# Reordering the attention steps beside an MLP's column blocks, with the first loads in halves (Trainium2, one core)

## The chip, the cores and the metric

One core of a Trainium2 chip runs the whole kernel. The metric is the device time of one execution in microseconds, lower is better. A profile of one more execution shows the engines: TensorE (PE, with weight loads as PEld), VectorE (DVE), ScalarE (ACT), GpSimd (POOL), SyncE (SP) and the DMA queues.

## The reference

```python
q, k, v: (8, 8, 576, 64)   # batch, heads, sequence, head size
kv = einsum('bhsd,bhse->bhde', k, v)
o  = einsum('bhsd,bhde->bhse', q, kv)
o  = o / sqrt(mean(o*o, -1) + 1e-6) * g_norm       # per head
x  = o.transpose(0, 2, 1, 3).reshape(4608, 512)
h  = x @ w_in                                      # 512 -> 2048
g  = max(h, 0) + alpha * min(h, 0)
out = g @ w_out                                    # 2048 -> 512, float32
```

Linear attention (no softmax) over 576 positions, a norm per head, and an MLP with a PReLU over all 4608 tokens.

## The kernel before

The 4608 tokens are cut into nine windows of 512 (`W`). A window needs the normed attention output transposed, 512 channels in four tiles of 128 (`xt`, one for each pair of heads), and then runs sixteen column blocks, called groups (`g`, 128 of the 2048 hidden columns each).

**The MLP.** `m1_group` (L325) runs four h matmuls (L310), one for each `xt` tile, into one of three PSUM buffers `h`; ScalarE makes `m_sb` (L317) and VectorE `gt` (L319) out of it. The y matmuls (`y_mm`, L332) of a window run one window later, four in each group beside the h matmuls; `y_out` copies a finished tile with ScalarE (L339) and sends it off. Window 0 is different: its h groups run alone (L367), and its y matmuls then run in a block of their own (L379), into four PSUM tiles `ya` to `yd`, three of which are `h` buffers.

**The attention.** For a batch b and a pair of heads j there are four steps. `step_t` transposes q (five matmuls, L222) into `qt_ps`, and VectorE copies it to `qt_sb` (L231). `step_kv` multiplies k and v (five matmuls, L237) into `kv_ps`, and VectorE masks it to `kv_sb` (L245). Both use the same single PSUM buffer (`ps_s`, tag "s"). `step_ot` multiplies both (L256) into `ot_ps` (two buffers), and ScalarE squares it (`sq_sb`, L262). `step_ssq` sums the squares (L268, one PSUM buffer); ScalarE takes Ln and Exp (L270, L273) and VectorE multiplies to `xt` (L275).

**The order.** Each engine works through its own instructions in the order in which the program was written (`manual_schedule`). `step_stream` (L280) gives the steps of all windows in one sequence: ot j-1, t j, ssq j-1, kv j. `attn_step` takes the next one. In windows 1 to 8 one step is taken behind each group (L406), so the sixteen steps for window w+1 end behind group 15 of window w. In the first y block one or two are taken behind each group from group 6 on. At the start, `keep_warm` (L198) puts matmuls whose result is not used between the steps.

**The loads.** GpSimd issues all loads of q, k, v and the weights, in one order. `load_main` brings 512 of a batch's 576 positions into a stage tile (two per tensor), `load_rem` the other 64 straight to their place; `regroup` copies the stage tile into the layout of the steps, on VectorE, ScalarE or GpSimd. For batch 0 the loads and regroups go by pairs of heads; the regroups of batch 1 are on VectorE (L371), and those of batch 2 and later on GpSimd, behind their loads.

Of the kernel before, what the change touches and what calls it, by code (L numbers as in the profile page):

```python
# [17 lines left out]
def kernel(  # L18
# [161 lines left out]

    for j in range(NPAIR):
        for nm in ("k", "v", "q"):
            load_main(0, nm, 2 * j, 2 * j + 2)
            if j == 0:
                load_rem(0, nm)
    for i in range(WQ):
# [7 lines left out]
    load_batch(2)  # L194
    regroup_batch(2)

# [20 lines left out]

    def step_t(b, j):
        qs = bufs[b % NBUF]["q"]
        qt_ps = ps_s.tile([P, NT * P], FP16, name="qt_ps", tag="s")  # L220
        for t in range(NT):
# [10 lines left out]

    def step_kv(b, j):
        ks, vs = bufs[b % NBUF]["k"], bufs[b % NBUF]["v"]
        kv_ps = ps_s.tile([P, P], FP32, name="kv_ps", tag="s")
        for t in range(NT):
            nc.tensor.matmul(  # L237
                out=kv_ps[:],
                lhsT=ks[:, t, 2 * j : 2 * j + 2, :],
                rhs=vs[:, t, 2 * j : 2 * j + 2, :],  # L240
                start=(t == 0),
                stop=(t == NT - 1),
            )
        kvs[b, j] = attn_p.tile([P, P], FP16, name="kv_sb", tag=f"kv{j}")
        nc.vector.tensor_mul(out=kvs[b, j][:], in0=kv_ps[:], in1=mask32[:])  # L245
# [33 lines left out]

    def step_stream():  # L280
        for w in range(NW):
            new = w < B
            for j in range(NPAIR + 1):
                if j > 0:
                    yield w, lambda: step_ot(w, j - 1)
                if new and j < NPAIR:
                    yield w, lambda: step_t(w, j)
                if j > 0:
                    yield (w + 1 if j == NPAIR else w), lambda: step_ssq(w, j - 1)
                if new and j < NPAIR:  # L290
                    yield w, lambda: step_kv(w, j)

    stream = step_stream()
    windows_done = 0

    def attn_step():
        nonlocal windows_done
        nxt = next(stream, None)
        if nxt is None:
            return False  # L300
        nxt[1]()
        windows_done = nxt[0]
        return True

# [49 lines left out]

    for j in range(NPAIR):
        regroup(0, "k", 2 * j, 2 * j + 2)
        regroup(0, "v", 2 * j, 2 * j + 2, nc.scalar)
        regroup(0, "q", 2 * j, 2 * j + 2)
        n = 3 if j == 0 else 4
        for _ in range(n):  # L360
            attn_step()
            keep_warm(2)
    while windows_done < 1:
        attn_step()
        keep_warm(1)

    for g in range(NF):  # L367
        m1_group(0, g)


    for nm in ("k", "v", "q"):  # L371
        regroup(1, nm, 0, H)
# [4 lines left out]
        ps_h.tile([P, W], FP32, name="yd", tag="h"),  # L377
    ]
    for g in range(NF):  # L379
        for a in range(TPW):  # L380
            y_mm(ys[a], 0, a, g)
        if g >= 6:
            attn_step()
        if g >= 10:
            attn_step()
    for a in range(TPW):
        y_out(ys[a], 0, a)
    while windows_done < 2:
        attn_step()

    for w in range(1, NW):
        if w + 2 < B:
            load_batch(w + 2)
            regroup_batch(w + 2)
        y = None
        for g in range(NF):
            m1_group(w, g)
            if w > 1:
# [5 lines left out]
                if part == TPW - 1:  # L404
                    y_out(y, w - 1, a)
            attn_step()  # L406
        while windows_done < min(w + 2, NW):
            attn_step()
    for a in range(TPW):
# [34 lines left out]
```

## Time and profile before

| | |
|---|---|
| runs of the kernel before | 339.92, 340.24, 340.5 us; median 340.24 |
| the profiled execution | 339.78 us, its span 338.0 us |
| TensorE busy | 300.1 us, 89% |
| VectorE busy | 159.7 us, 47% |
| ScalarE busy | 174.8 us, 52% |
| GpSimd busy | 84.3 us, 25% |
| granted TensorE clock, mean | 0.988 |

The span runs from the first to the last instruction. A matmul of 512 columns shows as 380 ns from its issue to its end, but the next one starts long before that; so what counts on TensorE is the distance of starts and the idle time ahead of an instruction, in brackets, with what ended it.

### The profile page before, as it was taken

The numbers are of one execution on the slowest core, as the hardware profiler recorded it, in microseconds if no ns is written. First come the engines' busy times: TensorE is split into PE (matmuls) and PEld (weight loads), VectorE is DVE, ScalarE is ACT, GpSimd is POOL, SyncE is SP. The second block draws the span as 40 slices with busy tenths as digits, with TensorE's granted clock in tenths as the row PEclk, the third lists the DMA queues.
The fourth block names the chain that finished last, engine by engine and source line by source line (L and its number), as shares of the span: only waits on it lengthen the run. The fifth ranks groups of instructions, "written<-read, shape, count | busy, mean of one in ns | idle before, by whom it ended". The sixth has DMA issues, their size and how long they took to land.

```text
span 338.0 us, 4258 instructions
## 1 busy us (share of the span) xinstructions
PE 300.1 (89%) x1614; PEld 143.8 (43%) x1614; DVE 159.7 (47%) x272; ACT 174.8 (52%) x293; POOL 84.3 (25%) x89
## 2 busy tenths in 40 slices
PE   5768998487779997999899989998998899999994
PEld 1333444243334544554454445444444444444441
DVE  5445842347645554554455445544554555444400
ACT  2356604557646664566456646563656684444411
POOL 9943417585752053305420000000000000000000
PEclk9799999989999999999999999999999999999999
DMA  8999997999391159204921111100001112100042
GB/s 79 171 204 200 197 195 91 157 190 178 40 178 39 31 64 195 46 32 65 192 48 33 31 31 33 31 33 32 31 33 31 31 32 49 46 31 33 32 94 62
DMA packets 47717, 28.07 MB, mean 83 GB/s; under 512 B 14400, under 2 KB 43088, under 8 KB 47696
## 3 DMA queue, kind: packets, MB, share of 16 engines
q0 software_dynamic: 42000, 18.35, 43.9%
q1 hardware_dynamic: 5696, 9.45, 9.9%
q8 instruction: 12, 0.20, 0.3%
q14 instruction: 9, 0.07, 0.1%
HBM read 36.71 MB, written 9.44 MB: 137 GB/s over the span
## 4 chain that ended last, share of the span: by engine, by line
PE 80%; ACT 9%; DVE 5%; POOL 2%; DMA 2%; issue 1%; POOLq 0%; ACTq 0%
PE h_ps L310 34%; PE y_ps L332 33%; DVE xt L275 3%; ACT rstd L270 3%; ACT rstd L273 3%; PE ot_ps L256 3%; PE qt_ps L222 3%; PE kv_ps L237 2%; PE ssq_ps L268 2%; DMA qst<-in_q_dram 2%; ACT y_sb L339 1%; ACT m_sb L317 1%; DVE gt L319 1%; PE yd L332 1%; PE ya L332 1%
## 5 line engine op out<-in xcount | busy, mean ns | idle before, releaser
L310 PE MATMUL h_ps<-xt,w_in_sb 128*128 128x512 f16 x576 | 147.6, 382 | 14.8 <-DVE xt L275 12.4
L319 DVE SCALAR_TENSOR_TENSOR gt<-m_sb,beta_sb,h_ps 128x512 f16<-128x512 f32 x144 | 107.4, 746 | 97.0 <-ACT m_sb L317 95.1
L332 PE MATMUL y_ps<-w_out_sb,gt 128*128 128x512 f16 x512 | 128.8, 379 | 0.0
L317 ACT ACTIVATE m_sb<-h_ps 128x512 f32<-128x512 f32 x144 | 85.3, 594 | 83.7 <-PE h_ps L310 83.2
L332 PEld LDWEIGHTS <-gt 128*128 128x128 f16 x576 | 55.9, 98 | 79.0 <-issue 14.0
L310 PEld LDWEIGHTS <-w_in_sb 128*128 128x128 f16 x576 | 54.0, 98 | 57.7 <-issue 6.1
L275 DVE SCALAR_TENSOR_TENSOR xt<-ot_ps,g2col,rstd 128x512 f16<-128x512 f32 x36 | 27.0, 751 | 46.4 <-ACT rstd L273 46.4
L262 ACT ACTIVATE sq_sb<-ot_ps 128x512 f16<-128x512 f32 x36 | 21.5, 597 | 35.7 <-PE ot_ps L256 35.5
L270 ACT ACTIVATE rstd<-ssq_ps,eps_t 128x512 f32<-128x512 f32 x36 | 24.8, 688 | 14.4 <-PE ssq_ps L268 14.4
L339 ACT COPY y_sb<-y_ps 128x512 f32<-128x512 f32 x32 | 18.7, 585 | 19.0 <-PE y_ps L332 19.0
L256 PE MATMUL ot_ps<-qt_sb,kv_sb 128*128 128x512 f16 (+7 forms) x64 | 15.2, 292 | 11.5 <-DVE kv_sb L245 11.5
L273 ACT ACTIVATE rstd<-rstd 128x512 f32<-128x512 f32 x36 | 22.7, 629 | 1.1
L231 DVE COPY qt_sb<-qt_ps 128x576 f16<-128x576 f16 x32 | 14.5, 453 | 10.0 <-PE qt_ps L222 10.0
L222 PE MATMUL qt_ps<-ident,qsb 128*128 128x128 f16 x160 | 14.5, 223 | 2.4 <-DVE qsb L139 2.2
L201 PE MATMUL warm_ps<-warm,mask 128*128 128x512 f16 x41 | 14.3, 454 | 2.3 <-DVE warm L95 2.3
L222 PEld LDWEIGHTS <-qsb 128*128 128x128 f16 x160 | 11.6, 99 | 10.7 <-DVE qsb L139 3.9
L139 POOL COPY ksb<-kst 128x2048 f16<-128x2048 f16 x6 | 11.4, 1893 | 18.2 <-DMA kst<-in_k_dram 18.2
L256 PEld LDWEIGHTS <-kv_sb 128*128 128x128 f16 x64 | 6.2, 97 | 21.9 <-DVE kv_sb L245 15.7
L237 PEld LDWEIGHTS <-ksb 128*128 128x128 f16 x160 | 11.7, 99 | 8.4 <-DVE qt_sb L231 0.6
L128 POOL DMA_DIRECT2D ksb<-in_k_dram x8 | 5.7, 713 | 37.5 <-PE kv_ps L237 35.7
L237 PE MATMUL kv_ps<-vsb,ksb 128*128 128x128 f16 x160 | 14.4, 222 | 0.4 <-DVE qt_sb L231 0.3
L268 PE MATMUL ssq_ps<-sq_sb,mask 128*128 128x512 f16 x36 | 13.7, 380 | 0.9 <-ACT sq_sb L262 0.9
(44 smaller groups left out, 126.5 us busy)
## 6 DMA issues: line engine op xcount, KB each, us to landing
out_dram<-y_sb SPq DMA_DIRECT2D x40, 128.0 KB, 2.3
out_dram<-y_sb SPq DMA_DIRECT2D x16, 256.0 KB, 2.2
kst<-in_k_dram POOLq DMA_DIRECT2D x7, 512.0 KB, 6.3
vst<-in_v_dram POOLq DMA_DIRECT2D x7, 512.0 KB, 8.8
qst<-in_q_dram POOLq DMA_DIRECT2D x7, 512.0 KB, 10.8
w_in_sb<-in_moe_w_in_dram POOLq DMA_DIRECT2D x4, 512.0 KB, 9.5
w_out_sb<-in_moe_w_out_dram POOLq DMA_DIRECT2D x4, 512.0 KB, 15.9
kst<-in_k_dram POOLq DMA_DIRECT2D x4, 128.0 KB, 4.8
```

Of the source, the lines that this page charges most:

```text
L222: nc.tensor.matmul(out=qt_ps[:, t * P : (t + 1) * P], lhsT=qs[:, t, 2 * j : 2 * j + 2, :], rhs=ident16[:], is_transpose=True, start=(t == ...
L237: nc.tensor.matmul(out=kv_ps[:], lhsT=ks[:, t, 2 * j : 2 * j + 2, :], rhs=vs[:, t, 2 * j : 2 * j + 2, :], start=(t == 0), stop=(t == NT - 1),)
L256: nc.tensor.matmul(out=ot_ps[:, n0 - w * W : n1 - w * W], lhsT=kvs[b, j][:], rhs=qts[b, j][:, n0 - b * S : n1 - b * S], start=True, stop=True,
L262: nc.scalar.activation(out=sq[:], in_=ot_ps[:], func=AF.Square)
L270: nc.scalar.activation(out=rstd[:], in_=ssq_ps[:], func=AF.Ln, bias=eps_t[:], scale=inv_d,)
L273: nc.scalar.activation(out=rstd[:], in_=rstd[:], func=AF.Exp, bias=0.0, scale=-0.5)
L275: nc.vector.scalar_tensor_tensor(out=xts[w, j][:], in0=ot_ps[:], scalar=g2col[:], in1=rstd[:], op0=ALU.mult, op1=ALU.mult,)
L310: nc.tensor.matmul(out=h_ps[:], lhsT=w_in_blk(c, g), rhs=xts[w, c][:], start=(c == 0), stop=(c == NC - 1),)
L317: nc.scalar.activation(out=m_sb[:], in_=h_ps[:], func=AF.Relu, scale=-1.0)
L319: nc.vector.scalar_tensor_tensor(out=gt[:], in0=m_sb[:], scalar=beta_sb[:, g : g + 1], in1=h_ps[:], op0=ALU.mult, op1=ALU.add,)
L332: nc.tensor.matmul(out=y[:], lhsT=gts[w, g][:, a * P : (a + 1) * P], rhs=w_out_blk(g), start=(g == 0), stop=(g == NF - 1),)
L339: nc.scalar.copy(out=y_sb[:], in_=y[:])
```

## The change

The sequence of the steps is written anew (`window_steps`): t j, ot j-1, kv j, ssq j-1, and the steps for window w+1 all stand in window w, spread so that the last comes behind group 13 instead of behind group 15. In window 1 they begin behind group 4. In the first y block steps stand between y matmuls, half a group apart, and end in group 14. Batch 0 is loaded in two halves of four heads, the remainders between them; the steps of two pairs run together, with three of their PSUM tiles taken from the `h` buffers, and the first three groups of window 0 run their matmuls for the early heads before the late heads are there. The regroup of batch 2 moves from GpSimd to VectorE, into window 1, and the load of batch 3 moves behind it in the program. Fewer `keep_warm` matmuls run at the start (10 + 10 instead of 10 + 31).

```diff
@@ -178,11 +178,12 @@
         i, r = divmod(g, GW)
         return w_out_sb[i][:, r, :]
 
-    for j in range(NPAIR):
-        for nm in ("k", "v", "q"):
-            load_main(0, nm, 2 * j, 2 * j + 2)
-            if j == 0:
-                load_rem(0, nm)
+    for nm in ("k", "v", "q"):
+        load_main(0, nm, 0, H // 2)
+    for nm in ("k", "v", "q"):
+        load_rem(0, nm)
+    for nm in ("k", "v", "q"):
+        load_main(0, nm, H // 2, H)
     for i in range(WQ):
         load_w_in(i)
     load_batch(1, ("k",))
@@ -192,7 +193,6 @@
     load_w_out(2)
     load_w_out(3)
     load_batch(2)
-    regroup_batch(2)
 
 
     def keep_warm(n):
@@ -215,9 +215,9 @@
 
     qts, kvs, xts = {}, {}, {}
 
-    def step_t(b, j):
+    def step_t(b, j, pool=(ps_s, "s")):
         qs = bufs[b % NBUF]["q"]
-        qt_ps = ps_s.tile([P, NT * P], FP16, name="qt_ps", tag="s")
+        qt_ps = pool[0].tile([P, NT * P], FP16, name="qt_ps", tag=pool[1])
         for t in range(NT):
             nc.tensor.matmul(
                 out=qt_ps[:, t * P : (t + 1) * P],
@@ -230,9 +230,9 @@
         qts[b, j] = attn_p.tile([P, S], FP16, name="qt_sb", tag=f"qt{j}")
         nc.vector.tensor_copy(out=qts[b, j][:], in_=qt_ps[:, 0:S])
 
-    def step_kv(b, j):
+    def step_kv(b, j, pool=(ps_s, "s")):
         ks, vs = bufs[b % NBUF]["k"], bufs[b % NBUF]["v"]
-        kv_ps = ps_s.tile([P, P], FP32, name="kv_ps", tag="s")
+        kv_ps = pool[0].tile([P, P], FP32, name="kv_ps", tag=pool[1])
         for t in range(NT):
             nc.tensor.matmul(
                 out=kv_ps[:],
@@ -277,30 +277,20 @@
             op0=ALU.mult, op1=ALU.mult,
         )
 
-    def step_stream():
-        for w in range(NW):
-            new = w < B
-            for j in range(NPAIR + 1):
-                if j > 0:
-                    yield w, lambda: step_ot(w, j - 1)
-                if new and j < NPAIR:
-                    yield w, lambda: step_t(w, j)
-                if j > 0:
-                    yield (w + 1 if j == NPAIR else w), lambda: step_ssq(w, j - 1)
-                if new and j < NPAIR:
-                    yield w, lambda: step_kv(w, j)
-
-    stream = step_stream()
-    windows_done = 0
-
-    def attn_step():
-        nonlocal windows_done
-        nxt = next(stream, None)
-        if nxt is None:
-            return False
-        nxt[1]()
-        windows_done = nxt[0]
-        return True
+    def window_steps(w):
+        f = []
+        for j in range(NPAIR):
+            f.append(("t", j))
+            if j > 0:
+                f.append(("ot", j - 1))
+            f.append(("kv", j))
+            if j > 0:
+                f.append(("ssq", j - 1))
+        f += [("ot", NPAIR - 1), ("ssq", NPAIR - 1)]
+        if w >= B:
+            f = [x for x in f if x[0] in ("ot", "ssq")]
+        fn = {"t": step_t, "kv": step_kv, "ot": step_ot, "ssq": step_ssq}
+        return [lambda n=n, j=j: fn[n](w, j) for n, j in f]
 
 
     gts = {}
@@ -352,23 +342,38 @@
             i += cnt
 
 
-    for j in range(NPAIR):
-        regroup(0, "k", 2 * j, 2 * j + 2)
-        regroup(0, "v", 2 * j, 2 * j + 2, nc.scalar)
-        regroup(0, "q", 2 * j, 2 * j + 2)
-        n = 3 if j == 0 else 4
-        for _ in range(n):
-            attn_step()
-            keep_warm(2)
-    while windows_done < 1:
-        attn_step()
-        keep_warm(1)
-
-    for g in range(NF):
+    H_POOL = (ps_h, "h")
+    for j0 in (0, 2):
+        regroup(0, "q", 2 * j0, 2 * j0 + 4)
+        regroup(0, "v", 2 * j0, 2 * j0 + 4, nc.scalar)
+        regroup(0, "k", 2 * j0, 2 * j0 + 4)
+        j1 = j0 + 1
+        step_t(0, j0, H_POOL)
+        step_t(0, j1, H_POOL)
+        step_kv(0, j0)
+        step_kv(0, j1, H_POOL)
+        step_ot(0, j0)
+        step_ot(0, j1)
+        if j0 == 0:
+            keep_warm(4)
+            step_ssq(0, j0)
+            step_ssq(0, j1)
+            keep_warm(6)
+    first = [ps_h.tile([P, W], FP32, name="h_ps", tag="h") for g in range(3)]
+    for g in range(3):
+        m1_mm(first[g], 0, g, (0, 1))
+    step_ssq(0, 2)
+    step_ssq(0, 3)
+    for g in range(3):
+        m1_mm(first[g], 0, g, (2,))
+    for g in range(3):
+        m1_mm(first[g], 0, g, (3,))
+        m1_evac(first[g], 0, g)
+    for g in range(3, NF):
         m1_group(0, g)
 
 
-    for nm in ("k", "v", "q"):
+    for nm in ("q", "k", "v"):
         regroup(1, nm, 0, H)
     ys = [
         ps_y.tile([P, W], FP32, name="ya", tag="y"),
@@ -376,24 +381,31 @@
         ps_h.tile([P, W], FP32, name="yc", tag="h"),
         ps_h.tile([P, W], FP32, name="yd", tag="h"),
     ]
+    steps = window_steps(1)
     for g in range(NF):
         for a in range(TPW):
             y_mm(ys[a], 0, a, g)
-        if g >= 6:
-            attn_step()
-        if g >= 10:
-            attn_step()
+            if g >= 6 and steps and (a == 1 or (a == 3 and g >= 8)):
+                steps.pop(0)()
     for a in range(TPW):
         y_out(ys[a], 0, a)
-    while windows_done < 2:
-        attn_step()
+    for f in steps:
+        f()
 
     for w in range(1, NW):
-        if w + 2 < B:
+        steps = window_steps(w + 1) if w + 1 < NW else []
+        n = len(steps)
+        first_g = 4 if w == 1 else 0
+        if 1 < w and w + 2 < B:
             load_batch(w + 2)
             regroup_batch(w + 2)
         y = None
         for g in range(NF):
+            if w == 1 and g == first_g - 1:
+                for nm in ("q", "k", "v"):
+                    regroup(2, nm, 0, H)
+                load_batch(3)
+                regroup_batch(3)
             m1_group(w, g)
             if w > 1:
                 a, part = divmod(g, TPW)
@@ -403,9 +415,10 @@
                     y_mm(y, w - 1, a, gg)
                 if part == TPW - 1:
                     y_out(y, w - 1, a)
-            attn_step()
-        while windows_done < min(w + 2, NW):
-            attn_step()
+
+            want = n * (g - first_g + 1) // (NF - 2 - first_g)
+            while steps and n - len(steps) < want:
+                steps.pop(0)()
     for a in range(TPW):
         y = ps_h.tile([P, W], FP32, name="y_ps", tag="h")
         for g in range(NF):
```

TensorE behind the last group that has attention steps, in window 2. First before (behind group 15; the rows at the end are window 3's group 0), where L332 are y matmuls, L268 is ssq and L310 are h matmuls:

```order
L332 LDWEIGHTS gt
L332 MATMUL y_ps<-w_out_sb_178,gt 128x512
L268 LDWEIGHTS mask_106
L268 MATMUL ssq_ps<-sq_sb,mask_106 128x512
L310 LDWEIGHTS w_in_sb_155
L310 MATMUL h_ps<-xt,w_in_sb_155 128x512
```

and of the change, behind group 13 of window 2 (L256 is ot 3, L300 are h matmuls):

```order
L322 LDWEIGHTS gt
L322 MATMUL y_ps<-w_out_sb_162,gt 128x512
L256 LDWEIGHTS kv_sb
L256 MATMUL ot_ps<-qt_sb,kv_sb 128x192
L256 LDWEIGHTS kv_sb
L256 MATMUL ot_ps<-qt_sb,kv_sb 128x320
L268 LDWEIGHTS mask_106
L268 MATMUL ssq_ps<-sq_sb,mask_106 128x512
L300 LDWEIGHTS w_in_sb_155
L300 MATMUL h_ps<-xt,w_in_sb_155 128x512
```

The last ssq stands two groups earlier, and directly behind the ot that it needs.

VectorE in the first y block (qt copy L231, kv_sb L245, xt L275), before, from the regroup of batch 1 on:

```order
L231 COPY qt_sb<-qt_ps 128x576
L245 TENSOR_TENSOR kv_sb<-kv_ps,mask_102 128x128
L231 COPY qt_sb<-qt_ps 128x576
L275 SCALAR_TENSOR_TENSOR xt<-ot_ps,g2col,rstd 128x512
L245 TENSOR_TENSOR kv_sb<-kv_ps,mask_102 128x128
L231 COPY qt_sb<-qt_ps 128x576
L275 SCALAR_TENSOR_TENSOR xt<-ot_ps,g2col,rstd 128x512
L245 TENSOR_TENSOR kv_sb<-kv_ps,mask_102 128x128
```

and of the change:

```order
L231 COPY qt_sb<-qt_ps 128x576
L245 TENSOR_TENSOR kv_sb<-kv_ps,mask_102 128x128
L231 COPY qt_sb<-qt_ps 128x576
L245 TENSOR_TENSOR kv_sb<-kv_ps,mask_102 128x128
L275 SCALAR_TENSOR_TENSOR xt<-ot_ps,g2col,rstd 128x512
L231 COPY qt_sb<-qt_ps 128x576
L245 TENSOR_TENSOR kv_sb<-kv_ps,mask_102 128x128
L275 SCALAR_TENSOR_TENSOR xt<-ot_ps,g2col,rstd 128x512
```

kv_sb j+1 now stands ahead of xt j, and the qt copy of pair j+2 behind it.

VectorE at the start of window 1, of the change (gt L309, regroup of batch 2 L139); before, these three copies were GpSimd's:

```order
L309 SCALAR_TENSOR_TENSOR gt<-m_sb,beta_sb,h_ps 128x512 x3
L139 COPY qsb_135<-qst 128x8x4x64
L139 COPY ksb_131<-kst 128x8x4x64
L139 COPY vsb_133<-vst 128x8x4x64
L309 SCALAR_TENSOR_TENSOR gt<-m_sb,beta_sb,h_ps 128x512 x2
L231 COPY qt_sb<-qt_ps 128x576
L309 SCALAR_TENSOR_TENSOR gt<-m_sb,beta_sb,h_ps 128x512
L245 TENSOR_TENSOR kv_sb<-kv_ps,mask_102 128x128
L231 COPY qt_sb<-qt_ps 128x576
```

The first qt copy of the window's steps stands behind three copies and gt 4, and kv_sb 0 and the second qt copy follow with one gt between.

## Rows read from the trace of the kernel before

**Rows 1.** Whom TensorE waited for in the whole span: us in total, times, longest us.

```profile
PE h_ps L310 <- DVE xt L275: 12.4, 7, 1.8
PE ot_ps L256 <- DVE kv_sb L245: 11.5, 9, 1.3
```

**Rows 2.** TensorE's timeline, windows 2 and 3: start us, us, engine, line, [idle before <-releaser].

```profile
94.88 0.38 PE L310 MATMUL h_ps<-xt,w_in_sb 128*128 128x512 f16 x1 [1.84 <-DVE xt L275]
...
121.66 0.44 PE L237 MATMUL kv_ps<-vsb,ksb 128*128 128x128 f16 x5
121.94 1.03 PE L310 MATMUL h_ps<-xt,w_in_sb 128*128 128x512 f16 x4
122.81 1.03 PE L332 MATMUL y_ps<-w_out_sb,gt 128*128 128x512 f16 x4
123.67 0.38 PE L256 MATMUL ot_ps<-qt_sb,kv_sb 128*128 128x192 f16 x2
...
125.83 0.81 PE L310 MATMUL h_ps<-xt,w_in_sb 128*128 128x512 f16 x3
128.49 0.38 PE L310 MATMUL h_ps<-xt,w_in_sb 128*128 128x512 f16 x1 [1.85 <-DVE xt L275]
```

**Rows 3.** Busy time by stage, first y block and window 1: us, engines, granted clock, DMA.

```profile
41.68:68.13 26.45, 18.95 (x117) 9.34 (x116) 8.99 (x17) 9.26 (x16) 13.33 (x12) 0.98 1.22 150
68.13:95.10 26.97, 20.93 (x121) 10.17 (x120) 16.68 (x28) 16.95 (x30) 18.29 (x17) 0.95 0.96 139
```

**Rows 4.** Timeline of all engines, one pair in the first y block.

```profile
57.36 0.38 PE L268 MATMUL ssq_ps<-sq_sb,mask 128*128 128x512 f16 x1
...
57.78 0.69 ACT L270 ACTIVATE rstd<-ssq_ps,eps_t 128x512 f32<-128x512 f32 x1 [0.76 <-PE ssq_ps L268]
...
58.50 0.63 ACT L273 ACTIVATE rstd<-rstd 128x512 f32<-128x512 f32 x1
...
59.83 0.28 DVE L245 TENSOR_TENSOR kv_sb<-kv_ps,mask 128x128 f16<-128x128 f32 x1
...
60.85 0.46 DVE L231 COPY qt_sb<-qt_ps 128x576 f16<-128x576 f16 x1 [0.74 <-PE qt_ps L222]
```

**Rows 5.** Timeline of all engines, end of the first y block.

```profile
64.31 0.36 PE L256 MATMUL ot_ps<-qt_sb,kv_sb 128*128 128x448 f16 x1 [1.25 <-DVE kv_sb L245]
...
64.71 0.60 ACT L262 ACTIVATE sq_sb<-ot_ps 128x512 f16<-128x512 f32 x1 [1.44 <-PE ot_ps L256]
65.36 0.38 PE L268 MATMUL ssq_ps<-sq_sb,mask 128*128 128x512 f16 x1 [0.69 <-ACT sq_sb L262]
...
68.13 1.44 PE L310 MATMUL h_ps<-xt,w_in_sb 128*128 128x512 f16 x3 [2.40 <-ACT y_sb L339]
```

**Rows 6.** The chain that ended last: start us, us, what; the longest load in it.

```profile
7.14 5.12 DMA qst<-in_q_dram
```

**Rows 7.** Timeline of all engines, the start.

```profile
8.38 0.45 PE L222 MATMUL qt_ps<-ident,qsb 128*128 128x128 f16 x5 [1.82 <-DVE qsb L139]
...
15.18 0.75 DVE L275 SCALAR_TENSOR_TENSOR xt<-ot_ps,g2col,rstd 128x512 f16<-128x512 f32 x1 [1.57 <-ACT rstd L273]
15.76 1.03 POOL L122 DMA_DIRECT2D kst<-in_k_dram  x1
```

**Rows 8.** TensorE's timeline, the h matmuls of window 0.

```profile
28.52 13.33 PE L310 MATMUL h_ps<-xt,w_in_sb 128*128 128x512 f16 x61 [1.36 <-DVE xt L275]
```

**Rows 9.** VectorE's timeline, three regroup copies.

```profile
12.28 0.29 DVE L139 COPY qsb<-qst 128x512 f16<-128x512 f16 x1 [1.38 <-DMA qst<-in_q_dram]
...
16.04 0.86 DVE L139 COPY ksb<-kst 128x512 f16<-128x512 f16 x1
...
43.18 0.69 DVE L139 COPY ksb<-kst 128x2048 f16<-128x2048 f16 x1
```

**Rows 10.** Busy time by stage, two stretches of one us (columns as in rows 3).

```profile
10.00:11.00 1.00, 1.00 (x4) 0.30 (x3) 0.77 (x2) 0.00 (x0) 1.00 (x3) 0.50 1.28 158
...
69.00:70.00 1.00, 1.00 (x5) 0.44 (x4) 0.00 (x0) 0.06 (x1) 0.53 (x1) 0.50 1.30 304
```

## The prediction, made blind

> **What bounds it now.** I read first for whom TensorE waited, then TensorE's timeline at a window's end, then the stages that differ from the steady one. A window is a block of 512 tokens. In windows 2 to 6 TensorE has no gap inside a window: each of sixteen groups is four h matmuls and four y matmuls, 1.73 us together (121.94 to 123.67, so 0.216 per matmul), and one attention step; kv takes 0.28 us of the queue [rows 2]. The only gap is at the start: the last matmul of group 0 stands 1.85 us for the last xt, at 94.88 and again at 128.49 [rows 2]. There are seven waits of this kind, 12.4 us [rows 1]: six at the starts of windows 2 to 7, and one of 1.36 us at the start of window 0 [rows 8]. The period is 33.61 us (94.88 to 128.49). The work in it is 16 x 1.73 = 27.65, and four head pairs at 0.28 (t) + 0.28 (kv) + 0.22 (ot) + 0.22 (ssq) = 4.0, together 31.65; so a boundary really costs 1.96. The second kind is ot waiting for kv_sb, 11.5 us in nine waits [rows 1], all before window 2, where less work stands between the steps. TensorE is the engine to count on, and every gap of it is paid in full.
>
> **Part 1, steady windows 2 to 6.** The last ssq moves from behind group 15 to behind group 13. From ssq's start over Ln and Exp to the end of xt it is 59.83 - 57.36 = 2.5 us [rows 4]; two groups are 3.46 us, so xt is there in time and the 1.96 goes. What is late next: sixteen steps must fit into fourteen groups, so two groups take two steps. Group 6 takes t 2 and ot 1, which need nothing fresh. Group 13 takes ot 3 and directly behind it ssq 3, which needs sq of that ot. The first y block had the same pair with nothing between: ot's second piece at 64.31, sq at 64.71, ssq at 65.36 [rows 5], 1.05 us from start to start, of which ot fills some 0.15. I take 0.9 lost per window (bounds 0.7, the idle time that the row names, and 1.5, were ScalarE still at Ln and Exp). Five windows: 5 x (1.96 - 0.9) = **5.3 us gained**. Window 7 has eight steps, none of them adjacent, and loses nothing, as before.
>
> **Part 2, first y block (41.68 to 68.13, 26.45 us [rows 3]).** Its work is 64 x 0.216 + 4.0 = 17.8. The steps are now spread by half groups and end at group 14. The waits of ot for kv_sb go, since kv j stands some 2 us ahead of ot j. But qt now stands behind xt in VectorE's order: ssq j is followed by t j+2, whose copy cannot start before xt j is done, 2.47 us after ssq, and takes 0.46 [rows 4]; kv j+2 shares the one PSUM buffer with qt and would start 2.0 us after ssq. So kv 2 and kv 3 wait 0.95 each. ssq 3 comes 1.3 us behind ssq 2 by the work between, but ScalarE must first do Ln (0.69), Exp (0.63) [rows 4] and sq (0.60) [rows 5]: it comes after 2.4, a wait of 1.1. The end: from ssq 3 over Ln, Exp and the copies of ya and yb to the next h matmul it is 68.13 - 65.36 = 2.77 [rows 5]; now ssq (0.22) and group 15's four y matmuls (0.86) lie inside, so 1.7 stay idle. The start keeps some 0.65, as yc and yd take over banks that h must leave: 17.8 + 0.65 + 3.0 + 1.7 = 23.2, **3.25 gained** (bounds: 1.5, if these waits are half as long again; 5, if qt does not queue behind xt).
>
> **Part 3, window 1.** Before, it ran from 68.13 [rows 3] to 94.23 (94.88 less three matmuls), 26.1, with 17.8 of work. Now no step runs in groups 0 to 3, and sixteen run in ten groups with no y matmuls beside them, while VectorE also takes over the regroup of batch 2 from GpSimd: three copies of 0.69 [rows 9], overlapping a little, 1.9 together, ahead of gt 3. VectorE has 16 gt of 0.75 (the form of xt [rows 7]), 4 x (0.46 + 0.28 + 0.75) and 1.9, together 19.8, more than TensorE's 17.8: this window becomes VectorE's. Walking through its order: t 0 waits 0.6 for the q copy; the qt copy stands behind gt 4 and ends 8.05 after the window's start, so kv 0 waits 2.05; t 1, directly behind kv 0, waits 0.75; t 2 0.7; kv 2 0.8; kv 3 1.0; ot 3 0.45; ssq 3 1.5. That is 7.85, so 25.65. The half clock at the window's start (granted 0.50 [rows 10], after the 2.40 us idle in rows 5) stays, as 1.7 and 1.1 idle now lie close together: later gt's there cost 0.9. And the fast copies can collide with GpSimd: a copy that takes 0.29 took 0.86 [rows 9] while GpSimd issued a DMA from 15.76 on [rows 7]; I add 0.3. Together 26.9, **0.8 lost** (bounds: 3 gained, if half of these waits vanish; 3 lost, if the clock falls again in the 2.05 us wait and the copies stand longer).
>
> By the Trainium skill ("SBUF — State Buffer", Who interferes with whom), a fast VectorE copy and a GpSimd instruction shut each other out for the whole instruction. The 0.86 us copy agrees with it. By it each of the three copies could stand for one whole copy of GpSimd: that is the second rival.
>
> **Part 4, start.** The first halves of k, v and q and the three remainders land together; the same bytes had landed at 7.14 + 5.12 = 12.26 before [rows 6], and the first pair's alone by 8.38 [rows 7]. I take 11.4, near the late end, since the queue is the same. One pair's chain took from 8.38 to the end of xt at 15.93, 7.55 [rows 7], partly at half clock (0.50 [rows 10]); two pairs together add one more Ln and Exp, 1.32: xt 1 is done at 20.3. Only then does VectorE reach the second regroup. The second double chain: copy 0.4, transposes 0.45, two qt copies 0.9, two kv_sb 0.57, ot 0.7, two sq 1.2, ssq 0.5, two Ln and Exp 2.64, xt 0.75: 8.1, so 28.4. The matmuls of the first three groups for the early heads run inside it. But all three h buffers are then held until VectorE empties them: 1.9 later (sum of a matmul, m, gt), at 30.3, group 3 starts, and 13 x 0.864 lead to the first y matmul at 41.5 against 41.68. **0.2 gained** (bounds: 2 gained, if the loads come a microsecond earlier and the clock is full; 2 lost, if the half clock also covers the first h matmuls). The removed warming matmuls ran in gaps and cost nothing; what they covered was the clock. The weight loads keep their order.
>
> By the Trainium skill ("TensorE: Matmul & The Clock Gate", Part 4: PE-mode transpose) transposes do not count as activity for the clock. The granted 0.50 at 10 us, after the first transposes, agrees with it. It speaks against replacing warming matmuls by longer runs of transposes: the slower rival below.
>
> **Sum.** 5.3 + 3.25 - 0.8 + 0.2 = 7.95. The profiled execution took 339.78 (its span of 338.0 and 1.8 around it); that gives 331.8. The median of the runs is 0.46 higher, so I forecast **332.3 us** (own range 330 to 334.5), chance 0.52.
>
> **Rivals.**
> - *The early steps are better hidden* (0.22): the waits of window 1 are half as long (3.9 us less) and the start runs at full clock (1.5 less). For: each of these waits stands on a fixed order that I walked with mean durations, and a short slip of one engine closes two of them. Against: the order itself. With half of both, 332.3 - 2.7 = 329.6, at best 327.
> - *Window 1 and the start are worse* (0.18): the three copies of batch 2 stand for GpSimd, the clock falls once more in the 2.05 us wait (1.7 us of lost work), and the start loses 0.5 to 2. For: rows 9 and 10. 332.3 + 3.9 = 336, up to 337.
> - *It does not do what it says* (0.03): ot 3 and ssq 3 give back the 1.96 in each window, if sq stands behind another full group's work on ScalarE. Then 332.3 + 5.3 = 337.6; with window 1 worse as well, 340, no change.
> - *Slower* (0.05): the clock stays at half through the h matmuls of window 0, because what goes before them is mostly transposes and waits. Against: those matmuls came after a stretch with gaps before, too, and 61 of them took 13.33 us [rows 8], full speed. At half, a matmul takes 0.216 more; all 64 cost 13.8, giving 346. It decides from 38 such matmuls on (8 us).
>
> About 0.2% (0.7 us) is what a measurement of this kernel can tell from no change. Faster by more: the first three cases, 0.92; within: 0.03; slower: 0.05. The range 327.5 to 336.5 takes in these three cases nearly to the ends of their bounds.
>
> **What would show it.** Right: no wait of h for xt at the starts of windows 2 to 7; one wait of ssq for sq of 0.7 to 1 us in each of windows 1 to 6, and a period of 32.55; kv waiting for the qt copy in the first y block and in window 1; first y matmul near 41.5; window 1 near 27 us long. Wrong: a period of 33.6, or one of 31.65 with ssq not waiting; window 1 at 23 or 30; first y matmul before 39 or after 44.

## The result: 329.69 us, and the profile after

The changed kernel takes 329.69 us (median of four runs, 328.09 to 329.94) against 340.08 for the kernel before beside it: a ratio of 0.9685, 95% interval 0.9651 to 0.9718, so faster by 10.4 us. The forecast was 332.3, range 327.5 to 336.5; its narrower range of 330 to 334.5 is missed by 0.3. The profiled execution's span went from 338.0 to 328.0 us. These 10.0 us are divided as follows; times are starts of h or y matmuls on TensorE, and a window's start is corrected for the wait of its fourth matmul, as in the prediction.

| stage | before | after | gained | forecast |
|---|---|---|---|---|
| start to the first y matmul | 41.68 | 39.09 | 2.59 | 0.2 |
| first y block | 26.45 | 23.37 | 3.08 | 3.25 |
| window 1 | 26.1 | 27.58 | -1.5 | -0.8 |
| windows 2 to 6, one period | 33.61 | 32.44 | 5 x 1.17 = 5.85 | 5.3 |
| window 7 to the end | 75.7 | 75.7 | 0.0 | 0 |

Whom TensorE waits for after the change (whole span: us in total, times, longest us), which answers to [rows 1]:

```profile
PE ssq_ps L268 <- ACT sq_sb L262: 5.5, 7, 1.2
PE qt_ps L222 <- DVE qsb L139: 4.8, 3, 2.9
PE kv_ps L237 <- DVE qt_sb L231: 4.7, 5, 1.9
...
PE h_ps L300 <- ACT y_sb L329: 1.5, 1, 1.5
PE h_ps L300 <- DVE xt L275: 1.5, 2, 1.1
...
PE ot_ps L256 <- DVE kv_sb L245: 0.3, 1, 0.3
```

The twelve microseconds of h waiting for xt are down to 1.5 (both inside the start), and those of ot for kv_sb to 0.3. In their place stand ssq waiting for sq, and kv waiting for the qt copy: the two new waits that the prediction named. The 4.8 of qt are waits for the regroup copies of q, 2.89 and 1.35 of them in the start and 0.59 in window 1.

TensorE's timeline at the end of window 2, which answers to [rows 2]:

```profile
117.76 0.38 PE L256 MATMUL ot_ps<-qt_sb,kv_sb 128*128 128x192 f16 x2
118.82 0.38 PE L268 MATMUL ssq_ps<-sq_sb,mask 128*128 128x512 f16 x1 [0.69 <-ACT sq_sb L262]
119.04 1.02 PE L300 MATMUL h_ps<-xt,w_in_sb 128*128 128x512 f16 x4
...
122.49 1.03 PE L300 MATMUL h_ps<-xt,w_in_sb 128*128 128x512 f16 x4
```

Window 3 starts at 122.49 and its four h matmuls stand together: xt was there. The price is the 0.69 us of idle time ahead of ssq 3 at 118.82, right behind its own ot.

The first y block and window 1 by stage (columns as in [rows 3]), and then TensorE's waits inside the first y block and up to the first h matmul of window 1:

```profile
39.09:62.46 23.37, 18.75 (x117) 9.37 (x116) 9.08 (x17) 9.15 (x16) 9.34 (x9) 0.99 1.49 190
62.46:90.04 27.58, 21.96 (x117) 10.43 (x116) 17.08 (x29) 16.13 (x29) 16.58 (x16) 0.88 0.78 113
```

```profile
53.01 0.44 PE L237 MATMUL kv_ps<-vsb,ksb 128*128 128x128 f16 x5 [0.80 <-DVE qt_sb L231]
...
56.68 0.44 PE L237 MATMUL kv_ps<-vsb,ksb 128*128 128x128 f16 x5 [0.80 <-DVE qt_sb L231]
...
59.69 0.38 PE L268 MATMUL ssq_ps<-sq_sb,mask 128*128 128x512 f16 x1 [0.84 <-ACT sq_sb L262]
```

```profile
62.46 6.01 PE L300 MATMUL h_ps<-xt,w_in_sb 128*128 128x512 f16 x20 [1.53 <-ACT y_sb L329]
```

Two waits of kv for the qt copy, one of ssq, and 1.53 us at the border, where [rows 5] had 2.40 behind a second wait of 0.69.

Window 1 on all engines: two of the three copies of batch 2, a DMA that GpSimd issues beside them, and three of the waits behind them:

```profile
68.07 0.93 DVE L139 COPY qsb<-qst 128x2048 f16<-128x2048 f16 x1
68.44 1.04 POOL L122 DMA_DIRECT2D qst<-in_q_dram  x1
...
68.93 1.05 DVE L139 COPY ksb<-kst 128x2048 f16<-128x2048 f16 x1
...
69.06 0.45 PE L222 MATMUL qt_ps<-ident,qsb 128*128 128x128 f16 x5 [0.59 <-DVE qsb L139]
...
72.31 0.62 PE L237 MATMUL kv_ps<-vsb,ksb 128*128 128x128 f16 x5 [1.93 <-DVE qt_sb L231]
...
88.10 0.38 PE L268 MATMUL ssq_ps<-sq_sb,mask 128*128 128x512 f16 x1 [1.21 <-ACT sq_sb L262]
```

The kv of the first pair waits 1.93 us for the qt copy, which stands behind the copies and gt 4, as walked through in the prediction (2.05). The granted clock is 0.88 over this window: it has two stretches at half clock (1.2 GHz, granted 0.50), one at its beginning and one from 72.5 to 75.5 us, behind the wait of kv 0.

The start: first the landing of the last remainder of the first half (from the chain that ended last), then all engines:

```profile
5.14 5.44 DMA qsb<-in_q_dram
```

```profile
9.87 1.57 PE L222 MATMUL qt_ps<-ident,qsb 128*128 128x128 f16 x10 [2.89 <-DVE qsb L139]
...
11.24 1.27 PE L237 MATMUL kv_ps<-vsb,ksb 128*128 128x128 f16 x10
...
17.74 0.75 DVE L275 SCALAR_TENSOR_TENSOR xt<-ot_ps,g2col,rstd 128x512 f16<-128x512 f32 x1 [0.49 <-ACT rstd L273]
18.41 0.42 DVE L139 COPY qsb<-qst 128x1024 f16<-128x1024 f16 x1
...
18.88 0.73 PE L222 MATMUL qt_ps<-ident,qsb 128*128 128x128 f16 x10 [1.35 <-DVE qsb L139]
...
19.45 0.72 PE L237 MATMUL kv_ps<-vsb,ksb 128*128 128x128 f16 x10
...
25.22 0.75 DVE L275 SCALAR_TENSOR_TENSOR xt<-ot_ps,g2col,rstd 128x512 f16<-128x512 f32 x1 [0.49 <-ACT rstd L273]
...
27.87 1.46 PE L300 MATMUL h_ps<-xt,w_in_sb 128*128 128x512 f16 x6 [1.03 <-DVE gt L309]
```

Ten transposes take 1.57 us at first and 0.73 later, ten kv matmuls 1.27 and 0.72: half clock over the first, full over the second. (The profile has no clock record before 14.4 us in this execution; the durations tell it.)

### The profile page after: what moved, and what is told of

Read it like the earlier page. It is cut to its first block, busy times and chain, and to the rows that moved or that the text cites. A ratio compares the mean times of both kernels' runs of the same rounds, so it can differ in the third digit from the quotient of the medians.

```text
span 328.0 us, 4205 instructions
## 1 busy us (share of the span) xinstructions
PE 298.4 (91%) x1593; PEld 143.7 (44%) x1593; DVE 160.2 (49%) x271; ACT 173.4 (53%) x291; POOL 74.7 (23%) x80
## 4 chain that ended last, share of the span: by engine, by line
PE 83%; ACT 7%; DVE 4%; DMA 2%; issue 1%; POOL 1%; POOLq 0%; ACTq 0%
PE h_ps L300 36%; PE y_ps L322 34%; PE kv_ps L237 3%; PE ssq_ps L268 2%; PE qt_ps L222 2%; PE ot_ps L256 2%; ACT rstd L270 2%; DMA qsb<-in_q_dram 2%; ACT rstd L273 2%; DVE xt L275 1%; DVE gt L309 1%; ACT sq_sb L262 1%; ACT m_sb L307 1%; PE yd L322 1%; DVE qt_sb L231 1%
## 5 line engine op out<-in xcount | busy, mean ns | idle before, releaser
L300 PE MATMUL h_ps<-xt,w_in_sb 128*128 128x512 f16 x576 | 147.3, 384 | 4.1 <-ACT y_sb L329 1.5
L309 DVE SCALAR_TENSOR_TENSOR gt<-m_sb,beta_sb,h_ps 128x512 f16<-128x512 f32 x144 | 106.8, 745 | 88.4 <-ACT m_sb L307 86.9
L300 PEld LDWEIGHTS <-w_in_sb 128*128 128x128 f16 x576 | 54.9, 99 | 67.2 <-issue 14.5
L275 DVE SCALAR_TENSOR_TENSOR xt<-ot_ps,g2col,rstd 128x512 f16<-128x512 f32 x36 | 27.0, 751 | 46.5 <-ACT rstd L273 46.5
L268 PE MATMUL ssq_ps<-sq_sb,mask 128*128 128x512 f16 x36 | 13.6, 378 | 7.0 <-ACT sq_sb L262 5.5
L231 DVE COPY qt_sb<-qt_ps 128x576 f16<-128x576 f16 x32 | 14.3, 451 | 6.4 <-PE qt_ps L222 6.3
L256 PE MATMUL ot_ps<-qt_sb,kv_sb 128*128 128x512 f16 (+7 forms) x64 | 14.2, 296 | 0.3 <-DVE kv_sb L245 0.3
L139 POOL COPY ksb<-kst 128x2048 f16<-128x2048 f16 x5 | 9.5, 1893 | 18.7 <-DMA kst<-in_k_dram 18.7
L139 POOL COPY qsb<-qst 128x2048 f16<-128x2048 f16 x5 | 9.5, 1894 | 7.4 <-DMA qst<-in_q_dram 7.4
L139 POOL COPY vsb<-vst 128x2048 f16<-128x2048 f16 x5 | 9.5, 1894 | 6.8 <-DMA vst<-in_v_dram 6.8
```

Source lines behind the costliest of these rows:

```text
L139: (eng or nc.vector).tensor_copy(out=dst, in_=src)
L256: nc.tensor.matmul(out=ot_ps[:, n0 - w * W : n1 - w * W], lhsT=kvs[b, j][:], rhs=qts[b, j][:, n0 - b * S : n1 - b * S], start=True, stop=True,
L275: nc.vector.scalar_tensor_tensor(out=xts[w, j][:], in0=ot_ps[:], scalar=g2col[:], in1=rstd[:], op0=ALU.mult, op1=ALU.mult,)
L300: nc.tensor.matmul(out=h_ps[:], lhsT=w_in_blk(c, g), rhs=xts[w, c][:], start=(c == 0), stop=(c == NC - 1),)
L309: nc.vector.scalar_tensor_tensor(out=gt[:], in0=m_sb[:], scalar=beta_sb[:, g : g + 1], in1=h_ps[:], op0=ALU.mult, op1=ALU.add,)
```

## Experiments

Ten kernels ran, each beside the kernel before. All start from the changed kernel, with its line names. In the expectations, e4's window 1 of "23.3" was read from group 1 to group 1; from start to start, as everywhere below, the same window is 22.4.

**The start alone undone** (e1_old_start): loads, regroups, steps and warming of the start as before.

```diff
-    for nm in ("k", "v", "q"):
-        load_main(0, nm, 0, H // 2)
...
+    for j in range(NPAIR):
+        for nm in ("k", "v", "q"):
+            load_main(0, nm, 2 * j, 2 * j + 2)
...
+    for j in range(NPAIR):
+        regroup(0, "k", 2 * j, 2 * j + 2)
+        regroup(0, "v", 2 * j, 2 * j + 2, nc.scalar)
+        regroup(0, "q", 2 * j, 2 * j + 2)
+        for _ in range(3 if j == 0 else 4):
+            a, b = seq.pop(0)
+            fn0[a](0, b)
+            keep_warm(2)
```

> The changed kernel with the start of the kernel before (loads and steps by pairs, 41 warming matmuls). Theory: the parts add up, so only the start moves: first y matmul at 41.7 instead of 39.1, everything later shifted by 2.6, so a span of 330.6 and a time near 332.3. Rival: a later start is absorbed in the first y block or in window 1, because these wait for loads: then under 1 us slower, 330.5.

330.98 us (330.90 to 331.37), 1.3 slower than the change, span 329.6. The first y matmul stands at 41.89, 2.8 later, as the theory says, and the y block is 23.38 long, so nothing waits for a load there. But 1.2 of the 2.8 come back in window 1, 26.39 instead of 27.58 (below: y block and window 1, then the first 20 h matmuls of window 1):

```profile
41.89:65.27 23.38, 18.75 (x117) 9.35 (x116) 9.09 (x17) 9.16 (x16) 9.35 (x9) 1.00 1.46 185
65.27:91.66 26.39, 20.66 (x117) 9.99 (x117) 17.09 (x29) 16.14 (x29) 16.75 (x16) 0.94 0.81 118
```

```profile
65.27 4.48 PE L299 MATMUL h_ps<-xt,w_in_sb 128*128 128x512 f16 x20 [1.54 <-ACT y_sb L328]
```

The granted clock in window 1 is 0.94 here and was 0.88: the stretch of half clock at its beginning did not come (20 h matmuls in 4.48 us, 6.01 in the change). So the parts do not simply add up, for a reason that neither theory named. The old start need not be what kept that stretch away: e2 and e3 have the change's code up to window 2, lack the stretch too, and their window 1 takes 25.76 and 26.45 us. Which part of the new start gains, the loads in halves or the paired steps, no run tells apart.

**The double steps moved apart** (e2_apart), in windows 2 to 6:

```diff
+    SPREAD = [1, 2, 3, 5, 6, 7, 8, 9, 10, 11, 13, 14, 15, 16, 16, 16]
...
+            if w > 1 and n == 16:
+                want = SPREAD[g]
```

> The changed kernel with the two groups of windows 2 to 6 that take two steps moved to groups 3 (ot 0, kv 1) and 10 (ot 2, kv 3), so that ot 3 and ssq 3 stand in different groups. Theory: the wait of ssq for sq is all that is left of the boundary, 0.8 us in each of five windows: period 31.65 instead of 32.45, time 4.0 less, about 325.7. Rival: the wait only moves (ssq 3 or kv 3 wait elsewhere, behind ScalarE's or VectorE's queue): period stays near 32.4 and the time at 329.7.

325.89 us (325.42 to 327.06), ratio to before 0.9577 (0.9554 to 0.96). The period is 31.60 us, all of it work. TensorE at the end of window 2:

```profile
117.52 0.38 PE L256 MATMUL ot_ps<-qt_sb,kv_sb 128*128 128x192 f16 x2
117.74 1.03 PE L300 MATMUL h_ps<-xt,w_in_sb 128*128 128x512 f16 x4
...
119.46 0.38 PE L268 MATMUL ssq_ps<-sq_sb,mask 128*128 128x512 f16 x1
119.68 1.03 PE L300 MATMUL h_ps<-xt,w_in_sb 128*128 128x512 f16 x4
```

With one group between ot 3 (117.52) and ssq 3 (119.46) neither has a wait. That is 5 x 0.84 = 4.2 in the windows; by the medians the time fell by 3.8. (In the profiled execution the first y matmul came 3.3 later than in the change's and window 1 was 1.8 shorter, both with the half clock falling elsewhere.) So the wait of ssq for sq was the whole rest of the boundary.

**The last ssq back to group 15** (e3_to_group15): the same edit with the table 1 to 16, so one step in each of the sixteen groups.

> The changed kernel with one step in each group of windows 2 to 6, in the new order, so that the last ssq stands behind group 15 as before. Theory: what counts is that the last ssq comes two groups early, not the new order: the wait of h for xt of about 1.85 us is back at the starts of windows 3 to 7, the wait of ssq for sq is gone, period 33.6, time 5 x 1.15 = 5.8 more, about 335.5. Rival: the new order itself shortens the chain, and the period stays under 32.6 with the time within 1 us of the changed kernel.

334.68 us (333.73 to 336.06), 5.0 slower than the change (5.8 by windows 2 to 6 alone; in the profiled execution the first y matmul came 0.7 earlier, at 38.39, and window 1 was 1.1 shorter). The period is 33.60, and the wait for xt is back (of the seven below, two are those of the start):

```profile
PE h_ps L300 <- DVE xt L275: 10.7, 7, 1.9
```

With the new order but the old end, the windows are as long as before. So the two groups ahead make the gain in windows 2 to 6, and the new order by itself gives nothing there.

**Window 1: copies on GpSimd, steps from group 0** (e4_w1_gpsimd), and **copies on GpSimd, steps from group 4** (e8_gpsimd_late):

```diff
     load_batch(2)
+    regroup_batch(2)
...
-        first_g = 4 if w == 1 else 0
+        first_g = 0
-        if 1 < w and w + 2 < B:
+        if w + 2 < B:
...
-            if w == 1 and g == first_g - 1:
-                for nm in ("q", "k", "v"):
-                    regroup(2, nm, 0, H)
-                load_batch(3)
-                regroup_batch(3)
```

> The changed kernel with the regroup of batch 2 on GpSimd behind its load, as before, and window 1's steps spread from group 0 on. Theory: window 1 is held by VectorE's order behind the three copies (kv 0 waits 1.9 us for the qt copy, t 0 waits 0.6, half clock follows); without them window 1 takes 24.5 to 25.5 us instead of 27.6, so 2 to 3 us less, about 327.2. Rival: VectorE's order among gt, qt and xt without y matmuls beside them is what holds it, wherever the steps begin: window 1 stays above 26.5 us and the time within 1 us of 329.7.

> As e4_w1_gpsimd (regroup of batch 2 on GpSimd) but window 1's steps again from group 4 on, sixteen in ten groups. It tells apart the two halves of what e4 undid. If VectorE's three copies were the price: kv 0 waits under 1 us, window 1 takes 24 to 25 us (e4 23.3). If squeezing the steps into ten groups was the price: window 1 takes 26 to 27.5 us, near the 27.6 of the change.

e4: 325.11 us (323.85 to 326.89), 4.6 faster than the change; e8, with the line on first_g as in the change: 325.36 (324.57 to 326.69). Window 1, first of e4, then of e8:

```profile
61.68:84.12 22.44, 18.42 (x116) 9.47 (x116) 14.58 (x26) 15.80 (x29) 12.19 (x10) 1.00 1.06 152
```

```profile
62.58:86.95 24.37, 20.43 (x116) 9.84 (x116) 14.86 (x26) 16.12 (x29) 13.52 (x11) 0.93 1.08 156
```

27.58 with both, 24.37 without the copies, 22.44 without the squeeze as well. So the copies on VectorE (with the load of batch 3 behind them) and what hangs on them cost about 3.2 us: in e8 kv 0 waits 0.69, not 1.93, and the second stretch of half clock does not come. That stretch stands behind kv 0 in all four profiles with the copies on VectorE (the change, e1, e2, e3; kv 0 waits 1.57 to 2.09) and in none of the seven with them on GpSimd. The other 1.9 is not the squeeze into ten groups alone, since e8 has the stretch of half clock at the beginning of the window and e4 has not:

```profile
62.58 6.05 PE L301 MATMUL h_ps<-xt,w_in_sb 128*128 128x512 f16 x20 [1.53 <-ACT y_sb L330]
```

The same 20 matmuls took 4.48 in e1, so up to 1.6 of the 1.9 is clock, and the squeeze costs between 0.4 and 1.9; no run has it without that stretch. In the times of e4 and e8 the difference is lost in the scatter of the start.

**Both together** (e5_both): e4, and e2's table for windows 1 to 6.

> The two edits that gained, together: the regroup of batch 2 back on GpSimd with window 1's steps from group 0, and the double steps of windows 1 to 6 at groups 3 and 10. Theory: they add up, since one acts in window 1 and the other in windows 2 to 6: period 31.6, window 1 below 23.3 us as its ssq 3 loses its 1.6 us wait; span 317 to 318, time near 320.5, and 4 to 5 below either alone. Rival: in window 1 the wait moves to kv or ot, window 1 stays at 23.3: 321.5.

322.28 us (319.45 to 322.99). The period is 31.60 and window 1 takes 22.21, 0.2 less than in e4: ssq 3 waits 0.74 there instead of 1.60, but another kv now waits for its qt copy (0.47). The time is 1.8 above what was expected, and 1.0 above what the gains of e2 (3.8) and e4 (4.6) would give together; the profile says where. The first y matmul stands at 41.93 in this execution and at 38.30 in that of e4, with the same code up to there. The stretch from 26 to 33 us in e5_both, in the change and, to look ahead, in f1_all (granted clock is the number behind POOL):

```profile
26.00:33.00 7.00, 6.04 (x15) 1.93 (x14) 3.47 (x6) 2.77 (x5) 1.97 (x3) 0.51 1.36 201
```

```profile
26.00:33.00 7.00, 5.94 (x27) 2.63 (x27) 5.05 (x7) 4.56 (x8) 2.20 (x4) 1.00 1.36 202
```

```profile
26.00:33.00 7.00, 6.11 (x29) 2.80 (x29) 5.90 (x9) 4.62 (x9) 3.06 (x4) 1.00 1.35 201
```

In e5_both the first h groups ran at half clock (0.51). In seven profiles with this start (the change, e2 to e5, e8 and e9) the first y matmul stands between 38.30 and 42.39. Five lie from 38.30 to 39.20; the two late ones, e2 and e5, are those with half clock on the first h matmuls. In these two the half clock over the first steps lasted longer as well (granted 0.51 and 0.80 from 13 to 20 us, 0.99 in e4): of the 3.6 us between e5 and e4, 1.4 are lost before the second transposes (19.49 against 18.09).

**Warming ahead of the first transposes** (e6_warm), on e5_both:

```diff
         j1 = j0 + 1
+        if j0 == 0:
+            keep_warm(14)
```

> The kernel of e5_both with 14 more warming matmuls ahead of the first transposes (result unused), where TensorE stands idle for 2.7 us. Theory: the half clock over the first steps comes from that idle time; filled, the transposes and kv of the first two pairs run at full clock (0.73 and 0.72 us for ten instead of 1.3 and 1.27), the first double chain ends 1 us earlier, and the later half clock seen in some runs (first y matmul between 38.3 and 42.4) does not come: first y matmul at 37 to 38, time 0.5 to 2 below e5_both. Rival: the transposes do not keep the clock up, whatever went before them: same half clock from 9 to 13 us, first y matmul at 38.3 or later, time as e5_both.

319.64 us (318.52 to 321.24), 2.6 below e5_both; some of that may be the scatter of the start just described. TensorE in the start:

```profile
6.71 3.19 PE L202 MATMUL warm_ps<-warm,mask 128*128 128x512 f16 x14
9.74 0.39 PE L223 MATMUL qt_ps<-ident,qsb 128*128 128x128 f16 x4
10.62 0.51 PE L223 MATMUL qt_ps<-ident,qsb 128*128 128x128 f16 x6 [0.49 <-DMA qsb<-in_q_dram]
10.97 0.72 PE L238 MATMUL kv_ps<-vsb,ksb 128*128 128x128 f16 x10
...
23.36 2.72 PE L301 MATMUL h_ps<-xt,w_in_sb 128*128 128x512 f16 x6 [1.07 <-DVE xt L276]
```

The ten kv now take 0.72 us instead of 1.27 and the ten transposes together 0.90 instead of 1.4: full clock, granted 1.00 up to 23 us. So what stands ahead of the transposes decides their clock, and filling the idle time there removes the half clock. But six h matmuls from 23.36 on took 2.72 us: a half-clock stretch behind the waits of the second half of the start. The first y matmul is at 37.95, and the runs still spread over 2.7 us.

**xt behind the qt copy** (e9_late_xt), on e5_both, in the first y block:

```diff
+                held, late_xt[:] = list(late_xt), []
+                if kind == "ssq":
+                    step_ssq(1, j, late=j < NPAIR - 1)
...
+                for f in held:
+                    f()
```

> The kernel of e5_both with one order changed on VectorE in the first y block: xt j of pairs 0 to 2 is issued behind the qt copy of the next t step instead of ahead of it. Theory of part 2: kv 2 and kv 3 wait 0.80 each because the qt copy stands behind xt; both waits go, the first y block takes 21.8 us instead of 23.4, the time is 1.6 below e5_both. Rival: kv waits for PSUM in any order, or ot waits for xt's late release of its PSUM tile: the block stays within 0.4 of 23.4.

318.19 us (317.74 to 321.72), 4.1 below e5_both. The order explains 1.9 of it; the rest goes with the start (first y matmul at 38.58 in the profiled execution, 41.93 in e5_both's). The block takes 21.47 us instead of 23.38; VectorE there:

```profile
50.66 0.46 DVE L232 COPY qt_sb<-qt_ps 128x576 f16<-128x576 f16 x1 [1.07 <-PE qt_ps L223]
51.33 0.75 DVE L280 SCALAR_TENSOR_TENSOR xt<-ot_ps,g2col,rstd 128x512 f16<-128x512 f32 x1 [0.22 <-ACT rstd L276]
...
53.38 0.46 DVE L232 COPY qt_sb<-qt_ps 128x576 f16<-128x576 f16 x1 [1.07 <-PE qt_ps L223]
```

The qt copy at 50.66 no longer stands behind xt, and kv has no wait left in this block. The order on VectorE was the cause.

**All that gained** (f1_all): e9_late_xt, e6's 14 matmuls, and 8 more in the waits of the second half of the start; and **the 8 alone** (f2_fill_late):

```diff
     step_ssq(0, 2)
+    keep_warm(3)
     step_ssq(0, 3)
+    keep_warm(4)
     for g in range(3):
         m1_mm(first[g], 0, g, (2,))
+    keep_warm(1)
```

> Everything that gained, together: e9_late_xt, the 14 warming matmuls of e6_warm ahead of the first transposes, and 8 more in the waits of the second half of the start (3 behind ssq 2, 4 behind ssq 3, 1 behind the matmuls for head pair 2; results unused). Theory: what differs from run to run is the half clock in the first 35 us, and with TensorE kept busy there no half clock falls ahead of the first y matmul: first y matmul at 37 to 37.5, span 314 to 315, time near 316.5. Rival: the warming matmuls stand ahead of needed work in TensorE's queue and cost what they save: first y matmul at 38 or later, time at 318 as e9_late_xt.

> As f1_all without the 14 warming matmuls ahead of the first transposes: only the 8 in the second half of the start. It tells apart which of the two fills matters. Theory: the half clock over the first transposes and kv stays and costs about 1 us (first y matmul at 38.3 to 39), but no half clock falls on the first h matmuls, so the runs lie within 1 us of each other, at 317.5 to 318.5. Rival: the late half clock has nothing to do with the waits in the second half: runs still spread over 3 us or more.

f1: 316.94 us (316.79 to 317.28), ratio to before 0.9321 (0.9308 to 0.9333). f2: 318.31 (318.08 to 318.80). With the late fill the runs of a kernel lie within 0.5 and 0.7 us of each other instead of 1.6 (e2) to 4.0 (e9), as the theory says. The mean granted clock of each run fits it: in e9 0.991 to 0.997 in the three runs from 317.74 to 318.58, and 0.972 in the one at 321.72. So most of the scatter was the half clock on the first h matmuls. The early fill adds another 1.4. The first y matmul of f1 stands at 38.11, not at 37 to 37.5: in that execution the first remainder of q landed later, and the transposes that need it started at 11.08 (in e6 at 10.62). f1_all is the fastest of all; by the medians it is 12.75 us below the change (kernel before: 340.1 beside both).

What f1 still waits for:

```profile
PE kv_ps L238 <- DVE qt_sb L232: 2.9, 4, 1.3
...
PE ssq_ps L271 <- ACT sq_sb L263: 1.6, 2, 0.8
PE h_ps L310 <- ACT y_sb L339: 1.5, 1, 1.5
```

What is left, besides the start, is kv behind the qt copy in window 1, two waits of ssq for sq (0.84 in the first y block, 0.74 in window 1), and the border of window 1 (1.53).

## Why the prediction was right

The time lies in the range, but 2.6 below the forecast, and at the 329.6 of the first rival. In the profiled execution the gains add up to 10.0, against 7.95 in the forecast: the start gave 2.4 more than its term and windows 2 to 6 0.55 more, the first y block and window 1 0.9 less. Windows 2 to 6 and the y block came as reasoned; window 1 came close partly by luck, as two errors there offset each other.

- **Part 1** held. The period was forecast as 32.55 and is 32.44: the 1.96 is gone, 0.84 came back. e3 shows that the early end makes the gain, e2 that ot 3 and ssq 3 side by side make the rest. The estimate of 0.9 came from one such pair in [rows 5]; its idle time there, 0.69, is what the new row shows too. The rival by which the whole 1.96 comes back is answered by this.
- **Part 2** held: 23.2 forecast, 23.37 measured. kv waits 0.80 twice by the row (0.95 forecast), ssq 3 0.84 (1.1), the border 1.53 (1.7). e9 shows the cause of the first two. What the rows name as idle is less than the time lost: the 0.69 ahead of ssq 3 in windows 2 to 6 was worth 0.84 in e2. How much of the 3.08 is the new order and how much the spread by half groups, no run tells apart.
- **Part 3** was right in kind: 26.9 forecast, 27.58 measured, but by two errors that offset each other. The first waits came as walked through (t 0 0.59, kv 0 1.93); the later ones were shorter (t 1 0.38 for 0.75, kv 2 0.55 for 0.8, kv 3 0.64 for 1.0, ssq 3 1.21 for 1.5), so that all together name 5.6 us, not 7.85. The half clock cost more than the 0.9 allowed: 1.5 on the first 20 h matmuls alone (6.01 against 4.48 in e1), and a second stretch behind the long wait of kv 0, which stood only in the bounds. Nor did the window become VectorE's: VectorE was busy 17.08 of 27.58 us, not 19.8. It cost time by its order, not by its load. Two of the copies took 0.93 and 1.05 instead of 0.69 while GpSimd issued DMAs; the third, with none beside it, took 0.67. By the Trainium skill ("SBUF — State Buffer", Who interferes with whom) a blocked copy would stand until the GpSimd instruction that came first is over. The second copy began at 68.93 beside an issue that ends at 69.48 and took 0.36 longer, less than the 0.55 left of it. The 0.86 us copy of [rows 9], which the prediction took as agreeing, was likewise held up by 0.57 where 0.75 were left of the issue in [rows 7]. So what is seen here is part of an instruction each time, with GpSimd's spans being rough; no GpSimd copy met these copies, so for those no run here shows the rule.
- **Part 4** is the term that was mis-sized: 0.2 forecast, 2.59 measured. Three steps of it were each too long. The last remainder of the first half landed at 5.14 + 5.44 = 10.58 (taken 11.4); the first double chain took 7.91 from there to the end of xt 1 at 18.49 (taken 8.87); the second took 7.56, from 18.41 to 25.97 (taken 8.1). From then on it went as written: 1.9 to group 3 at 27.87, and 11.2 to the first y matmul. One pair's chain of before held a wait for a load, and I added a second pair to all of it: sq 0 was done at 12.02, but ssq 0 stood behind the transposes of the second pair and ran at 13.38 (kernel before):

```profile
11.42 0.60 ACT L262 ACTIVATE sq_sb<-ot_ps 128x512 f16<-128x512 f32 x1 [4.43 <-PE ot_ps L256]
...
12.63 0.48 PE L222 MATMUL qt_ps<-ident,qsb 128*128 128x128 f16 x5 [0.39 <-DVE qsb L139]
...
13.38 0.38 PE L268 MATMUL ssq_ps<-sq_sb,mask 128*128 128x512 f16 x1
```

The bounds, 2 gained to 2 lost, were too narrow at the upper end. The prediction's own sign of being wrong, a first y matmul before 39, was missed by 0.09 here and met by the same start in e3, e4 and e9 (38.39, 38.30, 38.58); e2 and e5, at 42.39 and 41.93, lie inside the bounds, on the losing side.

- **The rivals.** The first gave the measured number, but not by its mechanism: the start was better through earlier loads and shorter chains, with the first transposes still at half clock, and the shorter waits of window 1 were eaten up by the clock. Of the second rival, the second fall of the clock in window 1 came true. The half clock of the slower rival did strike the first h matmuls in two of the profiles (e2, e5), but only a stretch of them: the first y matmul came about 3 us late, not 13.8. By the Trainium skill ("TensorE: Matmul & The Clock Gate", Part 4: PE-mode transpose) transposes do not count as activity. No run here separates that from plain idle time: with the idle time filled, the transposes ran at full clock (e6, f1).

## What to carry to other kernels

Where an engine works through a written order, look at each producer and its consumer: a step that stands directly behind the one it needs costs its whole latency, however early both stand, and one group between them can cost nothing. Put the end of a chain ahead of its use by more than the chain's length, and do not queue a small copy that frees a shared buffer behind a long chain on the same engine. At a start made of waits, fill TensorE's idle time: here that brought 1.3 us by the median (318.19 to 316.94) and took most of the scatter between runs away. And before a difference of a microsecond or two is put down to an edit, look where the half clock fell in both profiles.

## What was not expected of the hardware

Half clock at the start is not a fixed cost. The same code reached the first y matmul at 38.30 to 42.39 us, depending on how long the half clock lasted over the first steps and on whether it fell on the first h matmuls (granted 0.51 and 0.55 between 26 and 33 us in the two late ones, 1.00 in the others). The beginning of window 1 is the same: with 1.53 or 1.54 us of idle time ahead of it in every profile of the changed kernels, it ran at half clock in the change, e6 and e8 and at full clock in the other eight. What decides between the two, no run here shows. In f1_all, whose longest idle time behind the first warming matmul is 1.53 us, the granted clock was full from 6 to 313 us.
